# Sending the last two output tiles in one transfer from a shared buffer

## The chip, the cores and the metric

The kernel runs on one core of one Trainium2 chip. The metric is the device time of one execution in microseconds (us), as the median of several runs. The span in a profile is about 1.8 us shorter than the device time of the same run, since it counts from the first to the last instruction of the program. Engines: PE is TensorE, PEld its weight loads, DVE is VectorE, ACT is ScalarE, POOL is GpSimd, SP is SyncE; a "q" behind a name is the engine's sequencer, which waits, branches and issues transfers.

## The reference

```python
def reference(A_x, A_wqkv, A_wo, B_x, B_wqkv, B_wo, gate_w):
    x = A_x                                   # (1, 2048, 512) bf16
    g = _sigmoid((x * gate_w).sum(-1, keepdims=True))
    a = _A_ref(x, A_wqkv, A_wo)               # full softmax attention, 32 heads of 16
    b = _B_ref(x, B_wqkv, B_wo)               # 8 keys per query, two positions apart
    return g * a + (1 - g) * b                # (1, 2048, 512) bf16
```

The output is 2048 rows of 512 numbers. The kernel makes it in 16 tiles of 128 rows, 128 KB each in bf16. The change concerns tiles 14 and 15.

## The kernel before

A small scheduler in Python decides, while the program is built, in which order the engines get their steps. The last two tiles have a routine of their own. Its eight groups of four matmuls add up one output tile in a bank of PSUM (`self.misc`), the last of them being the ones that need the last piece of attention. Then one engine copies the bank to SBUF, and the tile leaves.

```python
def outproj_last(self, st, i, norm):          # st = 14, 15; i = 0, 1
    ...
    def ev():
        if i % 2 == 0:                        # tile 14: VectorE copies, SyncE sends
            ob = self.wk.tile([P, D], BF16, name="ob", tag="ob")
            nc.vector.tensor_copy(out=ob[:], in_=self.misc[:])
            nc.sync.dma_start(out=self.o_dst[:, st, :], in_=ob[:])
        else:                                 # tile 15: ScalarE copies and sends
            ob = self.eg[:].bitcast(BF16)[:, 512 * (i // 2):512 * (i // 2) + 512]
            nc.scalar.copy(out=ob, in_=self.misc[:])
            nc.scalar.dma_start(out=self.o_dst[:, st, :], in_=ob)
```

`self.eg` is an old buffer of 128 x 512 float32 that nobody reads any more by then; seen as bf16 it holds two tiles.

The program does not end there. A flag, computed on the way, tells whether the fast method was numerically safe. Every engine loads it at the end and branches over a long second program, the exact fallback:

```python
_Fast(c1, tc, aps, flag).build()
cond = nc.values_load(flag[0:1, 0:1], min_val=0, max_val=1)
with tc.If(cond > 0, label="exact"):
    ...                                        # some 18,000 instructions of TensorE alone
```

Early in the program SyncE and ScalarE, and only they, are told where that branch will go:

```python
far = [ENG.SP, ENG.Activation]
zero = nc.values_load(self.wz[0:1, 0:2].bitcast(I32), engines=far, min_val=0, max_val=1)
tc.mark_branch_hint_location("exact", hint=zero, engines=far)
```

## Time and profile before

| | before |
|---|---|
| device time, median of the first 3 runs | 703.62 us (702.6 to 704.75) |
| span of the profiled run | 701.2 us |
| TensorE, ScalarE busy | 97% each |
| ScalarE's last eviction ends | 696.36 us |
| from there to the end ("the tail") | 4.81 us |

The lines themselves stand in the prediction. The tail is what to keep in mind: all compute is over at 696.36, and the change touches little else. In the tables below I therefore count from the end of ScalarE's last eviction. That makes profiles comparable whose bodies differ by up to 3 us (that eviction ends at 695.69 in one at a granted TensorE clock of 0.998, at 698.98 in one at 0.992): no matmul runs in the tail.

### The profile page before, as it was taken

The numbers are of one execution on the slowest core, as the hardware profiler recorded it, in microseconds if no ns is written. First come the engines' busy times: TensorE is split into PE (matmuls) and PEld (weight loads), VectorE is DVE, ScalarE is ACT, GpSimd is POOL, SyncE is SP. The second block draws the span as 40 slices with busy tenths as digits, with TensorE's granted clock in tenths as the row PEclk, the third lists the DMA queues.
The fourth block names the chain that finished last, engine by engine and source line by source line (L and its number), as shares of the span: only waits on it lengthen the run. The fifth ranks groups of instructions, "written<-read, shape, count | busy, mean of one in ns | idle before, by whom it ended". The sixth has DMA issues, their size and how long they took to land.

```text
span 701.2 us, 21328 instructions
## 1 busy us (share of the span) xinstructions
PE 679.4 (97%) x8556; PEld 218.0 (31%) x8556; DVE 651.8 (93%) x1093; ACT 680.5 (97%) x696; POOL 429.1 (61%) x364
## 2 busy tenths in 40 slices
PE   9999999999999999999998999999999999999996
PEld 4432222233322232223332223322333232232343
DVE  6999999997899999999999899999999999989983
ACT  6999999999999999999999999999999999999995
POOL 4766877766476455555456666666567564576681
PEclk9999999999999999999999999999999999999999
DMA  6001101000100100000103236356463554566531
GB/s 175 5 16 36 45 3 31 2 2 9 35 2 15 26 1 5 6 2 9 34 1 92 99 79 165 106 146 162 96 156 97 149 134 112 128 167 173 136 84 36
DMA packets 64489, 48.70 MB, mean 69 GB/s; under 512 B 22528, under 2 KB 64000, under 8 KB 64256
## 3 DMA queue, kind: packets, MB, share of 16 engines
q1 hardware_dynamic: 63680, 45.83, 25.2%
q8 instruction: 69, 1.13, 0.7%
q0 software_dynamic: 288, 1.05, 0.5%
q10 hardware_dynamic: 416, 0.39, 0.2%
q14 instruction: 36, 0.29, 0.2%
HBM read 39.85 MB, written 5.26 MB: 64 GB/s over the span
## 4 chain that ended last, share of the span: by engine, by line
PE 60%; ACT 22%; issue 6%; DVE 5%; DMA 3%; SPq 2%; POOL 1%; ACTq 0%; DVEq 0%; POOLq 0%
ACT pt L1926 22%; PE fps L1872 21%; PE fps L1645 20%; PE fps L895 15%; DVE yb L1564 2%; DMA vw<-v_dram 1%; PE fps L1857 1%; SPq L1328 1%; PE fps L1378 1%; DVE yb L1573 1%; DMA erb<-er_dram 1%; DVE prod L1229 1%; SPq L968 1%; DMA x_in<-in_A_x_dram 1%; ACT er L1248 0%
## 5 line engine op out<-in xcount | busy, mean ns | idle before, releaser
L1926 ACT ACTIVATE pt<-fps 128x1024 bf16<-128x1024 f32 (+1 forms) x682 | 674.5, 1141 | 7.8 <-PE fps L1872 5.6
L1564 DVE TENSOR_SCALAR yb<-fps 128x512 int16<-128x512 f32 x584 | 377.8, 681 | 18.4 <-PE fps L1872 15.3
L1872 PE MATMUL fps<-qm,kT 32*128 32x512 bf16 x1976 | 285.9, 383 | 12.6 <-ACT pt L1926 7.8
L1645 PE MATMUL fps<-pt,vaug 128*32 128x512 bf16 (+1 forms) x1562 | 234.7, 373 | 0.4 <-DVE yb L1564 0.4
L1571 POOL TENSOR_TENSOR yb<-yb,pc 128x1024 int32<-128x1024 int32 (+1 forms) x104 | 188.4, 1822 | 64.6 <-DVE yb L1573 15.2
L1645 PE MATMUL fps<-yb,vaugw 128*32 128x512 f16 (+1 forms) x1228 | 174.6, 375 | 0.6 <-POOL yb L1571 0.4
L1872 PEld LDWEIGHTS <-kT 32*128 32x128 bf16 x1976 | 80.9, 91 | 272.2 <-issue 267.2
L1573 DVE TENSOR_SCALAR yb<-yb 128x2048 int16<-128x2048 int16 (+3 forms) x206 | 132.5, 670 | 0.6
L1645 PE MATMUL fps<-yb,vaug 128*32 128x512 f16 (+1 forms) x614 | 113.0, 375 | 0.0
L1360 POOL TENSOR_TENSOR er<-er,vw 128x512 bf16<-128x512 bf16 x64 | 72.8, 1156 | 49.7 <-DVE yb L1573 30.6
L895 PE MATMUL fps<-xT,ww 128*32 128x512 bf16 (+2 forms) x1296 | 99.5, 380 | 0.2
L1360 POOL TENSOR_TENSOR erb<-erb,vw 128x512 bf16<-128x512 bf16 x64 | 72.5, 1156 | 38.4 <-DVE yb L1573 20.6
L1645 PEld LDWEIGHTS <-vaug 128*32 128x32 bf16 x2176 | 64.8, 94 | 81.6 <-issue 74.7
L1645 PEld LDWEIGHTS <-vaugw 128*32 128x32 bf16 x1228 | 45.1, 94 | 41.8 <-issue 35.1
L1229 POOL TENSOR_TENSOR prod<-bq,bk 128x512 bf16<-128x512 bf16 x32 | 34.3, 1075 | 31.4 <-DVE yb L1573 17.4
L895 PEld LDWEIGHTS <-ww 128*32 128x32 bf16 x1296 | 25.8, 95 | 31.6 <-issue 23.8
L1678 POOL TENSOR_TENSOR t<-t,rc 128x512 bf16<-128x512 f32 x15 | 15.8, 1056 | 27.0 <-DVE yb L1573 12.2
L930 POOL TENSOR_SCALAR vaugw<-vaug 128x128 bf16<-128x128 bf16 (+1 forms) x24 | 20.4, 852 | 18.5 <-DVE vaug L923 10.8
L1857 PE MATMUL fps<-qm,kz 128*32 128x512 bf16 x288 | 30.8, 383 | 0.6 <-DVE yb L1564 0.4
L1229 DVE TENSOR_TENSOR prod<-bq,bk 128x2048 bf16<-128x2048 bf16 x24 | 29.9, 1271 | 0.2
L1668 DVE STREAM_TRANSPOSE t<-fps 128x512 f32<-128x512 f32 x32 | 22.7, 708 | 2.3 <-PE fps L1645 1.9
L895 PE MATMUL fps<-woB,oB 128*32 128x512 bf16 x256 | 19.9, 382 | 0.0
(117 smaller groups left out, 306.0 us busy)
## 6 DMA issues: line engine op xcount, KB each, us to landing
vw<-v_dram SPq DMA_DIRECT2D x128, 128.0 KB, 3.2
er<-er_dram SPq DMA_DIRECT2D x128, 64.0 KB, 3.3
erb<-er_dram SPq DMA_DIRECT2D x128, 64.0 KB, 2.9
v_dram<-vs SPq DMA_DIRECT2D x16, 128.0 KB, 2.6
qm<-qs SPq DMA_DIRECT2D x112, 16.0 KB, 1.8
out_dram<-ob SPq DMA_DIRECT2D x13, 128.0 KB, 2.7
x_in<-in_A_x_dram SPq DMA_DIRECT2D x3, 512.0 KB, 6.2
ww<-in_B_wqkv_dram SPq DMA_DIRECT2D x12, 128.0 KB, 2.8
```

The lines of the kernel that those rows point to most:

```text
L895: self.nc.tensor.matmul(out=out_ps[32 * c:32 * c + 32, 0:n], lhsT=lhsT_of(c), rhs=rhs, start=start, stop=stop, tile_position=(0, 32 * c))
L930: return self.nc.gpsimd.tensor_scalar(out=self.vw4[k][:, KD.index(st), h0:h1, 0:DH], in0=self.vaug4[:, st, h0:h1, 0:DH], scalar1=PW_W[k], ...
L1229: return e.tensor_tensor(out=pr[m % 2][:, a:b], in0=bq[ct][:, a:b], in1=bk[ct][:, o + a:o + b], op=ALU.mult)
L1360: return nc.gpsimd.tensor_tensor(out=st_["erb"][m % 4][:, g, :], in0=st_["erb"][m % 4][:, g, :], in1=st_["vw"][m % 2][:, g, :], op=ALU.mult)
L1564: return nc.vector.tensor_scalar(out=self.yb[bt["buf"]][:, 0, i * 512:(i + 1) * 512], in0=bank[:], scalar1=A, scalar2=1024.0 * (15.0 + PW_ ...
L1571: return nc.gpsimd.tensor_tensor(out=y[:, k, 0:n].bitcast(I32), in0=y[:, 0, 0:n].bitcast(I32), in1=self.pc[:, k:k + 1].to_broadcast([P, n ...
L1573: return nc.vector.tensor_scalar(out=y[:, k, 0:n], in0=y[:, 0, 0:n], scalar1=float(round(1024.0 * (PW_S[k] - PW_S[0]))), scalar2=None, op0 ...
L1645: nc.tensor.matmul(out=out, lhsT=v, rhs=r, start=start, stop=stop, tile_position=(0, 32 * j))
L1668: nc.vector.transpose(out=self.t1[:, par].rearrange("p a b -> p (a b)"), in_=self.flex[acc[b]])
L1857: nc.tensor.matmul(out=dst[32 * c:32 * c + 32, :], lhsT=self.kz[:, j, KZ.index(kt), 32 * c:32 * c + 32], rhs=self.qm[(4 * ct + qc) % NQM][ ...
L1872: nc.tensor.matmul(out=dst, lhsT=self.kT[ct % 2][32 * j:32 * j + 32, kt * 128:(kt + 1) * 128], rhs=self.qm[(4 * ct + qc) % NQM][par][32 * ...
L1926: nc.scalar.activation(out=self.pt[pi[0]][pi[1]][:, 0:n * 512], in_=self.aslot[si][:, 0:n, :].rearrange("p a b -> p (a b)"), func=ACT.Exp, ...
```

## The change

The intent: one transfer in place of two, so one completion to wait for, with the two evictions still side by side. Both engines write halves of `self.eg`; whoever comes last sends both tiles from SyncE. Two conditions in the scheduler lose a clause.

```diff
         def ev():
-            if i % 2 == 0:
-                ob = self.wk.tile([P, D], BF16, name="ob", tag="ob")
-                nc.vector.tensor_copy(out=ob[:], in_=self.misc[:])
-                nc.sync.dma_start(out=self.o_dst[:, st, :], in_=ob[:])
-            else:
-                ob = self.eg[:].bitcast(BF16)[:, 512 * (i // 2):512 * (i // 2) + 512]
-                nc.scalar.copy(out=ob, in_=self.misc[:])
-                nc.scalar.dma_start(out=self.o_dst[:, st, :], in_=ob)
+            ob = self.eg[:].bitcast(BF16).rearrange("p (t n) -> p t n", t=2)
+            (nc.scalar.copy if i else nc.vector.tensor_copy)(out=ob[:, i, :], in_=self.misc[:])
+            self.out_left -= 1
+            if self.out_left == 0:
+                nc.sync.dma_start(out=self.o_dst[:, st - i:st - i + 2, :], in_=ob)
 ...
     def run(self):
+        self.out_left = 2
 ...
-            if batch is not None and p < N and p - 64 * batch["blk"] >= TUNE["dlast"]:
+            if batch is not None and p - 64 * batch["blk"] >= TUNE["dlast"]:
                 close_batch()          # the same in two places
```

More of the change, by code (lines that the diff above doesn't have):

```diff
@@ L1881, in emit_qk @@
                 d[2].end = t["PE"] + 0.25
-            if batch is not None and p < N and p - 64 * batch["blk"] >= TUNE["dlast"]:
+            if batch is not None and p - 64 * batch["blk"] >= TUNE["dlast"]:
                 close_batch()
```

## The prediction

> **What bounds the kernel now.** I read the page first: engines, then slices, then the chain of work that ended last.
>
> ```profile
> span 701.2 us, 21328 instructions
> PE 679.4 (97%) x8556; PEld 218.0 (31%) x8556; DVE 651.8 (93%) x1093; ACT 680.5 (97%) x696; POOL 429.1 (61%) x364
> ...
> PE 60%; ACT 22%; issue 6%; DVE 5%; DMA 3%; SPq 2%; POOL 1%; ACTq 0%; DVEq 0%; POOLq 0%
> ```
>
> TensorE and ScalarE are both busy 97% of the span; DMA holds 3% of the chain. So the body is bound by compute, and a change that touches only the last two output tiles can only move what comes after the last matmul. To size that stretch I asked for the merged timeline of the end, in order of time (start us, length us, what, and in brackets the idle time before it):
>
> ```profile
> 694.46 0.45 DVE L1698 STREAM_TRANSPOSE oT<-t 128x256 bf16<-128x256 bf16 x1
> 694.69 1.04 PE L895 MATMUL fps<-wAv,oT 128*32 128x512 bf16 x14
> ...
> 695.55 0.69 DVE L1473 CAST ob<-fps 128x512 bf16<-128x512 f32 x1 [0.65 <-PE fps L895]
> 695.77 0.59 ACT L1477 CAST eg<-fps 128x512 bf16<-128x512 f32 x1 [3.50 <-PE fps L895]
> 696.27 0.33 SPq L1474 DMA_DIRECT2D out_dram<-ob  x1
> 696.39 0.38 ACTq L1478 DMA_DIRECT2D out_dram<-eg  x1
> ```
>
> The two evictions already run side by side: VectorE 695.55 to 696.25, ScalarE 695.77 to 696.36. Each transfer is issued 0.03 us after its eviction (696.27 and 696.39). The compute is over at 696.36 and the span ends at 701.2, so 4.8 us of tail are the only stretch the change can work on, 0.7% of the run. The view of the busy time by stretch says what that tail holds (the columns are us, PE, PEld, DVE, ACT, POOL, clock, DMA share, GB/s):
>
> ```profile
> 696.40:697.20 0.80, 0.00 (x0) 0.00 (x0) 0.00 (x0) 0.00 (x0) 0.00 (x0) 1.00 0.15 47
> 697.20:698.40 1.20, 0.00 (x0) 0.00 (x0) 0.00 (x0) 0.00 (x0) 0.00 (x0) 1.00 0.67 210
> 698.40:699.40 1.00, 0.00 (x0) 0.00 (x0) 0.00 (x0) 0.00 (x0) 0.00 (x0) 1.00 0.04 13
> 699.40:701.20 1.80, 0.00 (x0) 0.00 (x0) 0.00 (x0) 0.00 (x0) 0.00 (x0) 0.68 0.05 14
> ```
>
> Four parts: some 0.8 us until the bytes flow, 1.2 us of real data, 1.0 us in which hardly anything moves although the second landing is not in yet, and 1.8 us of closing. The landings are in the DMA issues of that stretch (KB each, us from issue to landing):
>
> ```profile
> out_dram<-ob SPq DMA_DIRECT2D x1, 128.0 KB, 2.7
> out_dram<-eg ACTq DMA_DIRECT2D x1, 128.0 KB, 3.0
> ```
>
> So the first tile lands at 696.27 + 2.73 = 699.00 and the second at 696.39 + 2.95 = 699.34, which is the event that starts the closing 1.85 us. The completion marks in the trace show why they are slow: of the 16 marks of each transfer, 14 of the first are in by 697.98 and 13 of the second by 698.36; the rest straggle to 699.00 and 699.34. The cleanest earlier tile (issued at 688.59) was home in 1.71 us. The stragglers fall beside instruction fetches: three of 8 KB run at 697.21 (0.54 us), 697.95 (0.35 us) and 698.31 to 698.83 (0.52 us), and the last, 4-byte, packet of the second transfer starts at 698.83, as that fetch ends. What asks for the fetches is the branch that skips the fallback path:
>
> ```profile
> L750 PEldq COMPARE_BRANCH  x1: 3579/3579/3579, 695.6 to 695.6; - x1
> L750 DVEq COMPARE_BRANCH  x1: 72/72/72, 696.2 to 696.2; - x1
> L750 SPq COMPARE_BRANCH  x1: 70/70/70, 696.7 to 696.7; - x1
> L750 ACTq COMPARE_BRANCH  x1: 68/68/68, 697.2 to 697.2; - x1
> ...
> L750 DVEq EVENT_SEMAPHORE  x1: 21/21/21, 699.1 to 699.1; - x1
> L750 PEldq EVENT_SEMAPHORE  x1: 51/51/51, 699.3 to 699.3; - x1
> ```
>
> TensorE branches at 695.57 and goes on at 699.15, VectorE at 696.19 and goes on at 699.09. SyncE and ScalarE, which were given a hint at the start, don't stall. So three things end within 0.3 us of each other: VectorE's return (699.09), TensorE's (699.25, its first instruction there), the last landing (699.34).
>
> **What the Trainium skill says.** "DMA: Bandwidth & Descriptors", section "Anatomy of one DMA", puts the fixed cost of one transfer at about 2.0 us, mostly the write's receipt and not the bytes; that fit is for the GpSimd path, and here the cleanest 128 KB store from SyncE took 1.71 us whole, so the shape agrees and the figure is a little high. The same page, "Rules for kernel authors", says that spreading transfers over issuing engines brings no bandwidth since all use the same 16 DMA engines; the trace agrees, as the two tiles together flow at 280 to 340 GB/s. "Perfetto Trace Analysis", section "DMA Instruction — HWDGE (DVE, Sync)", says that the issue's recorded time ends before the data moves; here 0.33 us of issue against 2.73 us to landing. "Runtime: NRT & Kernel Launch", section "Instruction fetch mechanics", says that a taken branch out of the current window must fetch its target by DMA first; the 3.58 us branch on TensorE and the 8 KB instruction packets agree.
>
> **The change part by part.** With line numbers struck out, the built order of TensorE and GpSimd in the main path is the same instruction for instruction, and VectorE, ScalarE and SyncE differ only in the named rows at the end. So the dropped condition in the two closings of a batch changes nothing here: it could act only if a batch were still open once all items are drawn. Body: 0.0 us.
> 1. VectorE's eviction writes the first half of the old gate buffer and no longer a fresh output buffer. Same form, so 0.69 us as before. The wait for the old buffer's transfer goes; it was passed long before (the eviction is idle for TensorE, 0.65 us). 0.0 us.
> 2. ScalarE's eviction writes the second half. I checked its waits in the built program: the count of VectorE's semaphore is 1087 in both versions, so it does not wait for VectorE's write into the same buffer. Still 695.77 to 696.36. 0.0 us.
> 3. ScalarE's transfer is gone (0.38 us of issue). ScalarE reaches its branch 0.38 us earlier, and then only waits. 0.0 us.
> 4. SyncE's transfer now waits for both evictions: issue moves from 696.27 to 696.36 + 0.03 = 696.39, when ScalarE's was issued before. Against the transfer that ended last: 0.0 us, perhaps +0.03 for a hop across engines.
> 5. It carries 256 pieces of 1 KB for 128. The 256 KB load of the same shape at the start took 0.45 us to issue, so +0.07 us on 0.38. Each of 16 DMA engines gets 16 pieces; at the packets' median of 0.048 us that is 0.77 us, the sum of the two streams that shared these engines before. But the first 128 KB started 0.11 us earlier; estimated +0.1 us on the data's end.
> 6. One completion for two: one 4-byte mark per engine is dropped, and the stragglers must clear one stream only. An engine held by a fetch no longer alternates between two queues: estimated -0.2 us, uncertain.
> Without fetches this would land at 696.39 + 1.71 + 8 x 0.048 = 698.5; with them I add the 0.6 to 1.0 us by which the stragglers trailed and get 699.1 to 699.5, against 699.34.
> 7. Closing: the same semaphores are still waited for and cleared one by one, some 0.06 us each. 1.85 us as before.
> Sum: +0.03 + 0.1 - 0.2, about -0.1 us, in the noise of 701.
>
> **The rivals.** (a) The merged transfer escapes the fetches and lands near 698.5. For it: clean tiles land in 1.71 us. Against it: the branches of TensorE and VectorE stay, and so do their fetches; and TensorE returns only at 699.25. The closing walk reaches TensorE's semaphore 0.8 us after it begins, so at most some 0.8 us can be won: 702.8. (b) The longer single stream is worse: the early half used to start 0.11 us sooner on a second queue, and an engine hit by a fetch now has 16 pieces behind it. The slowest earlier tile took 4.03 us; that would be +1 us, 704.6. (c) ScalarE waits for VectorE because they share a buffer: 696.25 + 0.59 gives +0.5 us, 704.1. The unchanged wait count speaks against it. None comes near 2%, which is 14 us.
>
> **Range and chances.** Before is 703.62 us; with -0.1 I say 703.5. The tail can move it by -0.8 to +1.0, but three runs of before alone span 702.6 to 704.75, so the noise of two medians of three dominates: about 1.5 us either way, 702.0 to 705.0. Faster by over 2% 0.01, within 2% 0.98, slower 0.01.
>
> **What would show it.** Body: the timeline up to 695.7 shifts by less than run-to-run noise and both evictions still overlap. Step 4: SyncE's one issue starts 0.03 to 0.1 us after ScalarE's eviction. Step 5: its issue takes 0.35 to 0.5 us, its data ends about 2 us after it. Step 6: landing 2.7 to 3.1 us after issue; under 2.3 would be rival (a), over 3.5 rival (b). Rival (c) shows as ScalarE's eviction starting at VectorE's end. Closing: 1.8 to 1.9 us from landing to end. A change of more than 2 us would prove me wrong: then the body moved, through something the order of instructions doesn't show.

## The result, and the profile after

The changed kernel took 703.39 us as the median of 4 runs (703.05 to 704.62), the kernel before 704.18 us in 4 (702.6 to 704.84). A ratio here is the mean time of one kernel's fast runs over that of the other's of the same rounds, so not quite the ratio of these medians: it is 0.9995, with a 95% interval of 0.9973 to 1.0017. The same, as predicted, and within the predicted range.

The profile is less even. The span is 701.8 us against 701.2, and all of that difference is in the tail. Here is the timeline of the end, of the changed kernel, to be held against that of before in the prediction:

```profile
695.55 0.69 DVE L1472 CAST eg<-fps 128x512 bf16<-128x512 f32 x1 [0.66 <-PE fps L895]
695.76 0.59 ACT L1472 CAST eg<-fps 128x512 bf16<-128x512 f32 x1 [3.51 <-PE fps L895]
696.37 0.38 SPq L1475 DMA_DIRECT2D out_dram<-eg  x1
```

The evictions stand where they stood, to 0.01 us, after 695 us of identical work: the body did not move, and the shared buffer makes neither engine wait. The one transfer goes out at 696.37, 0.03 us after ScalarE's end. Its line among the DMA issues (KB each, us from issue to landing):

```profile
out_dram<-eg SPq DMA_DIRECT2D x1, 256.0 KB, 3.5
```

It lands at 696.37 + 3.54 = 699.92, where the later transfer of before had landed at 699.34: 0.58 us later. The branches of the changed kernel, in order of time, with their lengths in ns:

```profile
L750 PEldq COMPARE_BRANCH  x1: 4209/4209/4209, 695.6 to 695.6; - x1
L750 ACTq COMPARE_BRANCH  x1: 68/68/68, 696.1 to 696.1; - x1
L750 DVEq COMPARE_BRANCH  x1: 72/72/72, 696.2 to 696.2; - x1
L750 SPq COMPARE_BRANCH  x1: 70/70/70, 696.8 to 696.8; - x1
```

Two things moved. ScalarE branches at 696.1 and not at 697.2, 1.04 us earlier. And TensorE stands 4.2 us in its branch and not 3.6. With the branches, the instruction fetches moved. The traffic by queue, in the 0.8 us from 697.1 to 697.9 in which most of the output flows (packets, MB, share of 16 engines), first before, then after:

```profile
q1 hardware_dynamic: 133, 0.12, 46.6%
q10 hardware_dynamic: 114, 0.11, 41.8%
q14 instruction: 1, 0.01, 4.2%
```

```profile
q1 hardware_dynamic: 172, 0.18, 65.0%
q14 instruction: 2, 0.02, 9.5%
```

Queue 1 is SyncE's, queue 10 ScalarE's, queue 14 brings instructions. Before, one such fetch of 8 KB began among the data; after, two, at 697.22 and 697.24. In the same stretch the output's queues passed 247 packets before and 172 after; part of that is the later start, for the first output packet comes at 697.11 before and at 697.27 after. Not in this view, since it began earlier, is a 16 KB fetch on queue 8, also an instruction queue: from 696.61 to 697.60 before, from 696.62 to 698.22 after. It will matter more than the others. The question for the experiments is thus not why nothing was gained, which a tail of 0.7% explains, but why the tail got longer when I had expected it 0.1 us shorter, and whether this one profile means anything.

### The profile page after: what moved, and what is told of

Its sections match the earlier page's. It is cut to its first block, busy times and chain, and to the rows that moved or that the text cites. A ratio compares the mean times of both kernels' runs of the same rounds, so it can differ in the third digit from the quotient of the medians.

```text
span 701.8 us, 21325 instructions
## 1 busy us (share of the span) xinstructions
PE 679.5 (97%) x8556; PEld 218.2 (31%) x8556; DVE 651.8 (93%) x1093; ACT 680.6 (97%) x696; POOL 429.3 (61%) x364
## 4 chain that ended last, share of the span: by engine, by line
PE 55%; ACT 21%; DVE 9%; issue 6%; SPq 4%; DMA 3%; POOL 1%; DVEq 0%; ACTq 0%; POOLq 0%
ACT pt L1924 21%; PE fps L1870 19%; PE fps L1643 18%; PE fps L895 14%; DVE yb L1562 5%; DVE yb L1571 2%; SPq L1328 1%; DVE prod L1229 1%; SPq L962 1%; PE fps L1855 1%; PE fps L1378 1%; DMA vw<-v_dram 1%; DMA erb<-er_dram 1%; SPq L1354 1%; DMA er<-er_dram 1%
```

## The experiments

Twelve runs, in three groups on three chips. The four of the last group ran once each, so their state is unknown; I use their tails alone and not their times. The two views that I set against each other: **T1**, merging itself costs, because the first half waits for the second and all goes through one queue; **T2**, taking the transfer away from ScalarE lets ScalarE branch early, and its instruction fetch falls among the data. In the first group they were not yet separated and stand as rival M (merging costs in itself) against S (stragglers behind fetches, scattered by chance).

### Both kernels again

No edit. First the kernel before against itself:

> The kernel before, unchanged, run against itself: the control. Both theories expect a ratio of 1.000 and an interval that shows what five rounds can resolve (from the first runs, 702.6 to 704.84 us, I expect about plus or minus 0.2%). From its second profile I want the scatter of the tail: evictions ending within 0.05 us of 696.36; last landing of the two transfers 2.7 to 3.5 us after ScalarE's issue if the fetches of the branch target decide it by chance, and again 2.95 within 0.1 if the split form has a fixed landing.

Measured: ratio 0.9993, interval 0.9976 to 1.0011. So five rounds resolve about 0.2%, or 1.3 us. The spread within a kernel goes with the granted clock: of its six runs, the two at 0.995 had spans of 703.1 and 703.5 us, the four at 0.997 and 0.998 had 700.3 to 701.2. Tail: landing 3.15 us after ScalarE's issue, 5.01 us to the end.

> The changed kernel, unchanged. Theory S (the last landing is set by stragglers that stand behind the instruction fetches of the skipped branch, and these scatter by some 0.6 us from run to run whatever the form of the transfer): ratio 0.998 to 1.002, and a landing that differs from the 3.54 us of the first profile by some tenths, anywhere from 2.7 to 3.6. Rival M (one transfer of 256 pieces is slower in itself by 0.5 us): landing again 3.4 to 3.6 us after issue, span 0.5 us over that of the control.

Measured: ratio 1.0007, interval 0.9991 to 1.0024: the same. Landing 3.48 us after the issue, tail 5.39. Later, in the third group, once more:

> The changed kernel once more, for the scatter of its landing, which stood at 3.54 and 3.48 us after issue. If the merged form lands late for a fixed reason: 3.4 to 3.6 and tail 5.3 to 5.5. If the two were chance: anything from 2.7.

Measured: landing 3.40 us, tail 5.32. The landings of these profiles, before and then the two of after:

```profile
out_dram<-ob SPq DMA_DIRECT2D x1, 128.0 KB, 3.0
out_dram<-eg ACTq DMA_DIRECT2D x1, 128.0 KB, 3.2
```

```profile
out_dram<-eg SPq DMA_DIRECT2D x1, 256.0 KB, 3.5
```

```profile
out_dram<-eg SPq DMA_DIRECT2D x1, 256.0 KB, 3.4
```

Three landings of the merged form at 3.54, 3.48 and 3.40 us speak against S as I had written it, any value from 2.7. But the split form's three, 2.95, 3.15 and 3.38 (the last with the shared buffer, below), come close to them, so chance is not ruled out.

### Without the fallback

The flag's load, the branch, the fallback and the hint are taken out of both kernels. The result stays right for these inputs, but this is a probe and no candidate, for the fallback is part of what the kernel promises.

```diff
-        zero = nc.values_load(self.wz[0:1, 0:2].bitcast(I32), engines=far, min_val=0, max_val=1)
-        tc.mark_branch_hint_location("exact", hint=zero, engines=far)
 ...
-    cond = nc.values_load(flag[0:1, 0:1], min_val=0, max_val=1)
-    with tc.If(cond > 0, label="exact"):
-        tc.strict_bb_all_engine_barrier()
-        with ExitStack() as c2:
-            _build_exact(c2, tc, aps)
```

> The kernel before without the fallback and its branch (the result stays right for these inputs): no fetch of a branch target at the end. Theory S: the stragglers go, the later of the two transfers lands 1.9 to 2.1 us after its issue and the span falls by about 1 us (ratio about 0.9985). Rival M says nothing on this one. A third view, that the stragglers come from the write to DRAM itself, expects landings of 2.7 us or more as before.

> The changed kernel without the fallback and its branch. Theory S: lands 2.0 to 2.3 us after issue, within 0.2 us of the split form, span within 0.3 us of it. Rival M: still 0.5 us later than the split form without fallback. The view that merging saves a completion expects it 0.2 us or more earlier than the split form.

Measured, first the split form, then the merged:

```profile
out_dram<-ob SPq DMA_DIRECT2D x1, 128.0 KB, 1.7
out_dram<-eg ACTq DMA_DIRECT2D x1, 128.0 KB, 2.0
```

```profile
out_dram<-eg SPq DMA_DIRECT2D x1, 256.0 KB, 2.1
```

No instruction packet is recorded in these tails, and the stragglers are gone: all 16 completion marks of the merged transfer come between 1.96 and 2.15 us, where the changed kernel's went from 1.98 to 3.54. Counted from ScalarE's eviction, the landing is at 2.01 us in the split form and 2.17 in the merged, and the tails are 3.02 and 3.25. So three things are shown, the first two by one profile of each form. The branch, with the fetches that follow it, delays the landing by 1.0 to 1.4 us. Merging without them costs 0.17 us, not 0.5 (rival M) and not minus 0.2 (the saved completion). And the flag's load, the branch and the fallback together are dear: ratios of 0.9966 (0.995 to 0.9983) and 0.9972 (0.9953 to 0.999) to the kernel before. I had expected 0.9985: the landing's 1 us came as expected, but the walk from landing to end shrank too, from 1.83 and 1.89 us to 1.02 and 1.08.

### Two transfers, both from SyncE

The changed kernel's buffer, each half sent by SyncE as soon as it is filled.

```diff
-            self.out_left -= 1
-            if self.out_left == 0:
-                nc.sync.dma_start(out=self.o_dst[:, st - i:st - i + 2, :], in_=ob)
+            nc.sync.dma_start(out=self.o_dst[:, st, :], in_=ob[:, i, :])
```

> The changed kernel's shared buffer, but two transfers of 128 KB, both from SyncE, each as soon as its half is filled. ScalarE branches early as in the changed kernel; the first half leaves early as in the kernel before. So it parts the 0.4 to 0.6 us by which the merged form lands later. Theory T1 (what costs is that the first half waits for the second): tail after ScalarE's eviction 4.8 to 5.0 us, like the split form. Theory T2 (what costs is that ScalarE's branch and with it its instruction fetch move forward into the data): tail 5.4 us, like the merged form. SyncE issues them one after the other, so the second goes out at 696.6 or so, 0.2 us later than from ScalarE: that adds up to 0.2 us to either.

Measured: ratio 0.9996 (0.9977 to 1.0015), tail 5.04, landing 3.21 us after ScalarE's eviction. This looks like T1, but the run does not settle it. The second issue took 1.51 us where the first took 0.33, so SyncE itself branched only at 699.76, and its fetch left the data window. ScalarE's early branch put a second 8 KB fetch at 0.88 us after the eviction, but the next one came only at 2.99, against 1.60 and 1.95 in the kernel before: fewer fetches met the data, not more, and the second half's data started late. Inconclusive.

### One transfer, from ScalarE

```diff
-                nc.sync.dma_start(out=self.o_dst[:, st - i:st - i + 2, :], in_=ob)
+                nc.scalar.dma_start(out=self.o_dst[:, st - i:st - i + 2, :], in_=ob)
```

> The changed kernel with its one transfer issued by ScalarE and not by SyncE: ScalarE branches late again (about 0.4 us after the issue), and SyncE, which then has nothing to do after 691, branches 5 us before the end, so that its fetch is long over. T1: landing still 0.2 us or more later than the split form's 2.95 to 3.15 after issue, tail 5.2 to 5.5. T2: ScalarE's fetch is back behind the data and SyncE's is gone, so landing 2.7 to 3.0 after issue and tail 4.6 to 4.9.

Measured: ratio 1.0003 (0.9985 to 1.002), landing 3.09 us after issue, tail 5.01. Between the two expectations, in neither. It speaks against a fixed cost of merging of 0.4 us and more: the same 256 pieces in one queue land 0.3 to 0.45 us sooner than from SyncE, now that ScalarE branches at 696.60, 0.85 us after its eviction, and its fetch starts as the bulk is through (1.99 us after the eviction, against 0.89 in the changed kernel). SyncE's fetch is gone from the window as well, and the 16 KB fetch on queue 8 ended 0.07 to 0.39 us sooner, so the run does not say which of the three did it. (The trace does not name the engine that asked for a fetch. I take the 8 KB ones from the branches: in every profile in which ScalarE branches early, and in no other, two start about 0.9 us after the eviction and not one, or with the hints, 0.8 and 1.0.)

### The hint for TensorE and VectorE too

```diff
-far = [ENG.SP, ENG.Activation]
+far = [ENG.SP, ENG.Activation, ENG.PE, ENG.DVE]
```

> The kernel before, with the hint of the branch's target given to TensorE and VectorE too, as SyncE and ScalarE have it[...]. If the stragglers and the long branch come from those two engines' fetches at the end: TensorE's branch falls from 3.6 us to under 0.5, the later landing to 2.0 to 2.4 us after issue, tail to about 4.0, and the time by 0.8 us, ratio 0.999. If a following block is fetched all the same (SyncE and ScalarE seem to fetch 8 KB after their branches in spite of the hint), the stragglers stay and the tail falls by 0.3 us at most. A hint that disturbs TensorE's own instruction stream would show as a longer body, evictions ending after 696.5 at the same clock.

> The changed kernel with the same two hints. If the fetches of TensorE and VectorE make the stragglers, landing 2.2 to 2.6 us after issue and 0.2 us behind the split form with hints, as without a fallback (2.15 against 1.98); tail about 4.2. If not, 3.2 to 3.5 as before.

Measured on the split form: TensorE's branch is

```profile
L750 PEldq COMPARE_BRANCH  x1: 504/504/504, 697.1 to 697.1; - x1
```

and so 3.1 us shorter, and yet the landing is at 2.82 us and the tail 4.67, 0.1 to 0.6 us less than without the hint. The 16 KB packet after TensorE's branch is still in the trace (at 698.30, 1.2 us after the branch): the hint takes away the standstill, but a block is fetched all the same, and the landing stays late. On the merged form: landing 3.28, tail 5.20. The ratios are 1.0008 (0.9994 to 1.0021) and 1.0006 (0.9991 to 1.0021): no gain in time that five rounds can see, if anything the wrong sign. The main expectation of both runs, a landing of 2.0 to 2.6 us, was wrong, and the case named beside it held: a following block is fetched all the same and the stragglers stay. The merged form was 0.5 us behind the split one here too.

### One transfer from SyncE, and ScalarE kept busy

This run was meant to part T1 from T2. SyncE's transfer is that of the changed kernel; ScalarE sends 1 KB to a scratch place, which holds its sequencer until its eviction is done and 0.5 us longer.

```diff
                 nc.sync.dma_start(out=self.o_dst[:, st - i:st - i + 2, :], in_=ob)
+                scr = self.tc.dram_tile([1, D], BF16, name="scr_dram")
+                nc.scalar.dma_start(out=scr[:], in_=ob[0:1, 1, :])
```

> The changed kernel, and ScalarE also sends 1 KB of the buffer to a scratch place in DRAM after its eviction: next to no data, but ScalarE reaches its branch late, as in the kernel before (about 697.1 instead of 696.1), with SyncE's transfer unchanged. T2 (the earlier branch of ScalarE puts its fetch among the data): ScalarE's fetch starts 1.6 us or more after the eviction instead of 0.9, landing of the 256 KB 3.0 to 3.2 us after issue, tail 4.9 to 5.1. T1 (the first half's late start, or the single queue): landing 3.4 to 3.6 and tail 5.4 as in the two profiles of the changed kernel.

Measured: the issues, ScalarE's branch, and the landing:

```profile
698.98 0.38 SPq L1475 DMA_DIRECT2D out_dram<-eg  x1
698.98 0.51 ACTq L1477 DMA_DIRECT2D scr_dram<-eg  x1
```

```profile
L750 ACTq COMPARE_BRANCH  x1: 68/68/68, 700.4 to 700.4; - x1
```

```profile
out_dram<-eg SPq DMA_DIRECT2D x1, 256.0 KB, 2.8
```

With an extra transfer the tail was shorter: landing 2.83 us after issue, tail 4.68 us, against 3.40 to 3.54 and 5.32 to 5.46 of the changed kernel. ScalarE branches 1.41 us after its eviction, and the last fetch before the landing starts 2.53 us after it, with the bulk through; the one before starts at 1.92, near the end of it. SyncE's transfer and branch are as in the changed kernel. So the fixed parts of T1, one queue and a late first half, do not by themselves cost 0.4 us: this run has both. It fits T2 but does not show it. It is one profile, better than T2 had asked for; ScalarE's branch came later than I had meant (0.8 us after the eviction, as before); and more than that branch differs. The 16 KB fetch ended 1.20 us after the eviction here, and 1.55 to 1.87 us after it in the changed kernel. The section "The tails side by side" shows what that is worth.

### The last transfer left out

Wrong on purpose: the two tiles are made and not sent.

```diff
-            if self.out_left == 0:
+            if self.out_left == 9:
```

> Wrong on purpose: the last two tiles are evicted and not sent. It tells what the end would be without their landing. If the landing sets the end and TensorE's return from its branch stands close behind, the tail is 3.9 to 4.4 us: TensorE's fetch, now undisturbed, takes 1.0 us and TensorE returns about 2.6 us after the eviction. If the return set the end in the changed kernel, the tail would stay at 5.0 or more.

Measured: tail 3.95 us, within the expectation. TensorE comes back from its branch 2.8 us after the eviction, VectorE at about the same time, and no landing is left to wait for. So, with the branch as it stands, I expect no way of sending the last tiles to make the tail shorter than about 3.9 us: the changed kernel's 5.39 holds 1.4 us that a transfer could give back, the kernel before 1.1.

### The shared buffer alone

```diff
-            self.out_left -= 1
-            if self.out_left == 0:
-                nc.sync.dma_start(out=self.o_dst[:, st - i:st - i + 2, :], in_=ob)
+            (nc.scalar if i else nc.sync).dma_start(out=self.o_dst[:, st, :], in_=ob[:, i, :])
```

> One part of the change alone: VectorE and ScalarE fill one buffer, but each half leaves at once by the queue of before (SyncE, ScalarE). The buffer should cost and bring nothing: evictions overlap as before, landing of the later transfer 2.9 to 3.2 us, tail 4.8 to 5.1. If sharing the buffer made one eviction wait for the other, ScalarE's would start 0.5 us later.

Measured: the evictions overlap as before (694.89 to 695.58 and 695.11 to 695.69), so the buffer costs the evictions nothing. But the landing was at 3.38 us and the tail 5.24, above what I had given as the upper end. In form this is the kernel before, so it widens that kernel's scatter.

### The tails side by side

All times in us after the end of ScalarE's last eviction; each number is from one profile, in the order in which the first column names them.

| kernel | 16 KB fetch ends | last landing | end of span |
|---|---|---|---|
| before: first, again, shared buffer alone | 1.24, 1.45, 1.68 | 2.98, 3.18, 3.41 | 4.81, 5.01, 5.24 |
| after: first, again, third | 1.87, 1.55, 1.65 | 3.57, 3.50, 3.43 | 5.46, 5.39, 5.32 |
| two from SyncE | 1.37 | 3.21 | 5.04 |
| one from ScalarE | 1.49 | 3.12 | 5.01 |
| one from SyncE, ScalarE busy | 1.20 | 2.85 | 4.68 |
| hints: split, merged | 1.21, 1.29 | 2.85, 3.30 | 4.67, 5.20 |
| no fallback: split, merged | none | 2.01, 2.17 | 3.02, 3.25 |
| not sent | 1.26 | none | 3.95 |

The second column is the one 16 KB fetch that meets the output. It starts 1.0 to 1.3 us after TensorE's branch begins, so I read it as TensorE's. Neither the prediction nor T1 and T2 reckoned with it. What such a fetch does to a transfer stands earlier in every trace, with no branch near. Tiles 12 and 13 are sent by SyncE one after the other, 128 KB each. In all 14 profiles no fetch is beside tile 12, and it lands 1.69 to 1.71 us after its issue. One 16 KB fetch is beside tile 13 (in 12 of the 14, no other fetch), and it lands after 2.91 to 3.80 us, always 1.11 to 1.18 us after that fetch ends. In the kernel before, tile 13:

```profile
q1 hardware_dynamic: 144, 0.13, 9.8%
q8 instruction: 1, 0.02, 2.5%
out_dram<-qs SPq DMA_DIRECT2D x1, 128.0 KB, 3.8
```

Of its 144 packets 135 start within 1.34 us of the issue, and 15 of its 16 completion marks are in by 1.69. The other nine packets, a sixteenth of them and so the share of one DMA engine, start from 2.60 on; the fetch ends at 2.61. So here one engine sends nothing of the tile until the fetch is through, and the last mark waits for it.

The tail fits this: in the three profiles of the split form the last landing comes 1.74, 1.74 and 1.73 us after the end of the 16 KB fetch. All of their scatter is in that fetch, which took 0.99, 1.20 and 1.42 us. The next 16 KB fetch, after the landing, when no output flows, scatters too: 0.96 to 1.36 us in the ten profiles that have one. In the merged form the distance is 1.70, 1.95 and 1.78 us, with ScalarE busy 1.66, and 1.63 sent from ScalarE.

The means of the three tails are 5.02 and 5.39: the merged form's is 0.37 us longer, or 0.05% of the run, and the three of one form only just do not overlap the three of the other. In the times it can't be seen. Of the 0.37 us, 0.06 lie after the landing and 0.31 before it. Of these, 0.24 go with a later end of the 16 KB fetch, and nothing here ties that to merging; 0.07 are left. Likewise the run with ScalarE busy landed 0.65 us before the mean of the changed kernel, and 0.50 of that is the earlier end of the fetch. With the hints, where the fetches ended at 1.21 and 1.29, the merged form still landed 0.45 us later. So what ScalarE's early branch costs lies between nothing and some 0.4 us and is not shown. No run changed the length of the 16 KB fetch alone.

## Why the prediction was right or wrong, point by point

The time and the class were right, and for the reason given: the change works on a tail of 4.8 us at the end of 701, so it can't reach 2%. That 703.5 fell within 0.2 us of the measured 703.39 is luck: four runs of one kernel span 2 us, and the tail moved the other way.

- **Where the stragglers come from: fetches, but not those that were named.** This is the reading that failed. It blamed three 8 KB fetches, the last because the last packet of the second transfer starts as that fetch ends (698.83). In the second profile of the kernel before, that packet starts 0.39 us after the end of the last such fetch, and the landing keeps its distance of 1.74 us to the 16 KB fetch, which the prediction left out. Its own trace showed what that costs, in tile 13. It added 0.6 to 1.0 us for stragglers; the changed kernel landed 1.26 to 1.40 us later than the merged form without a fallback.
- **Body, 0.0 us: right.** The evictions stand at the same place to 0.01 us in the first two profiles.
- **Steps 1 and 2, evictions and buffer, 0.0: right**, in the changed kernel and with the buffer alone.
- **Step 3, ScalarE's transfer gone, "ScalarE reaches its branch 0.38 us earlier, and then only waits. 0.0 us": wrong in its first half.** It came 1.04 us earlier: the removed transfer had also held ScalarE's sequencer until the eviction was done, and without it the flag's load ran beside the eviction, at 695.77. Its 8 KB fetch moved among the output's packets with it. Whether the 0.0 us is wrong too is not shown: putting a late branch back gave a tail of 4.68 for 5.39, in one profile, and most of that goes with the 16 KB fetch.
- **Step 4, issue 0.03 us after the eviction: right** (0.026).
- **Step 5, +0.1 us for the late first half: right in kind, a little small.** The issue took 0.38 us, in the range given; without fetches the merged form lands 0.17 us later. But the mark that its data ends about 2 us after the issue missed: in the first profile the last data packet starts 3.03 us after it.
- **Step 6, -0.2 us for the saved completion: wrong in sign.** I said that an engine held by a fetch no longer alternates between two queues. In the changed kernel's trace the last 13 data packets start one after the other, 0.04 to 0.09 us apart, the last at 3.05 us after the eviction, when all else is done: the look of one engine working off its backlog. The trace does not name the engine of a packet, so here that is a reading; in tile 13 the count of nine packets bears it out.
- **Step 7, closing 1.85 us: nearly.** It is 1.83 in the split form and 1.89 in the merged one, in all three profiles of each. SyncE goes through the transfers' semaphores in a fixed order at 0.07 us each, and the merged transfer's stands one place earlier, with one more to come after it. In the run with ScalarE busy, which moved it back by one place, it is 1.83 again.
- **The marks that I had set.** A landing over 3.5 us was to show rival (b), the worse single stream. It was 3.54, 3.48 and 3.40: (b) came nearest, with some 0.6 of its +1 us at most. Rival (a) did not happen, and its bound holds: the tail without any transfer is 3.95 us. Rival (c) did not happen.

The sum of -0.1 us measured as +0.37 in the means of three profiles. Without fetches +0.17 is the landing and +0.06 the order of semaphores; with them 0.24 goes with the end of the 16 KB fetch. These don't add up to one figure, as which fetches meet the data differs in each form. How much each single fetch costs in the tail stays open, and so does whether a fourth profile of each form would keep the 0.37.

No version with the fallback in place beat both in time. Their shortest tails with the output sent, 4.67 and 4.68, are single profiles, and the one that was timed in five rounds gave 1.0008.

## What to carry to other kernels

Before making the end of a kernel neater, ask how long the end is: a tail of 0.7% can't pay at 2%, and five rounds here resolve no better than 0.2%. When a transfer is taken away from an engine, its sequencer runs on, and what it does next, here a branch and a fetch, may share the DMA engines with the transfer that sets the end. When a transfer lands late, look at every packet that was in flight with it, the instruction queues' too, and look for an earlier transfer of the same kind with and without that company: tiles 12 and 13 would have told this before any run. Halves that are ready at different times may leave at different times; one completion for two saved nothing here.

## What the Trainium skill lacked or had wrong

- "Runtime: NRT & Kernel Launch", "Instruction fetch mechanics", has the stall of a taken branch, but not that the fetch slows other transfers. Here the last landing of 128 KB came 2.01 us after the eviction without the branch's fetches and 2.98 to 3.41 with them, that of 256 KB 2.17 and 3.43 to 3.57. A 16 KB fetch with no branch near did the same to tile 13: 2.91 to 3.80 us to landing for 1.69 to 1.71.
- The same section gives 16 KiB as the size of a refill. Here TensorE's packet after its branch has 16,384 bytes, and each packet on queue 14 at the end has 8,192.
- No page that I read says what a branch hint does not save: with it TensorE's branch took 0.50 us for 3.58, but a 16 KB packet still came 1.2 us after it.
- "DMA: Bandwidth & Descriptors", "Anatomy of one DMA", fits the fixed cost for the GpSimd path alone. From SyncE a store of 128 KB took 1.69 to 1.73 us to its last completion with no fetch and no other transfer beside it, and one of 256 KB 2.15 us.
- No page that I read says when an issue to a queue that is still busy takes longer. Here the second of two 128 KB stores from SyncE took 1.51 us to issue, the first 0.33 us; the run does not show why.
